# K and V held with 32 keys of two kv-heads per partition, moved by one transfer for each partition quadrant

## The chip, the cores and the metric

The kernel runs on one core of one Trainium2 chip. The metric is device time in microseconds (us), less is better. A core has five engines that run side by side and meet at semaphores: TensorE (PE in the profile, its weight loads PEld), VectorE (DVE), ScalarE (ACT), GpSimd (POOL) and SyncE (SP). Transfers between HBM and the on-chip memory SBUF are issued from a queue of SP, POOL or ACT and are carried out by 16 DMA engines that all queues share. SBUF has 128 partitions; a "quadrant" in this document is a block of 32 partitions in a row (0 to 31, 32 to 63, and so on). Matrix results land in PSUM, from which ACT or DVE copies them to SBUF ("evacuation").

## The reference, cut to what matters

Forward and backward pass of one decode step: attention over a window of a K/V cache and a gated feed-forward net in parallel on the same normalised input, summed with the input.

```python
B, Sq, D = 4, 1, 512
Hq, Hkv, Sk, Dh = 32, 8, 4096, 128          # W = Sk // 4 = 1024 keys are attended
...
q = (xn @ wq).reshape(B, Sq, Hq, Dh).transpose(0, 2, 1, 3)
k = repeat(k_cache[:, :, Sk - W:, :], 4, axis=1)
v = repeat(v_cache[:, :, Sk - W:, :], 4, axis=1)
p = softmax(einsum("bhqd,bhkd->bhqk", q, k) * Dh ** -0.5)
o = einsum("bhqk,bhkd->bhqd", p, v)
out = x + o.reshape(B, Sq, Hq * Dh) @ wo + (gelu(xn @ w_gate) * (xn @ w_up)) @ w_down
# returned: out, and the gradients of x, k_cache, v_cache, wq, wo, w_gate, w_up, w_down
```

The gradients of `k_cache` and `v_cache` (out_2, out_3) have the caches' full shape: 4 batches of 8 heads with 4096 keys. Only the last 1024 keys have a gradient; the 3072 in front of them are written as zeros. All arrays are bfloat16.

## The kernel before, in words

**Data moved.** By the issues of the profile: 32 transfers of 1.5 MB that write zeros, 16 loads of 1 MB (K and V, two for each batch of each), 16 stores of 1 MB (their gradients), 8 stores of 1 MB (gradients of wo and wq), 6 stores of 0.875 MB (gradients of the feed-forward weights), and 13.25 MB of weights.

**Who issues what.** SP loads the weights and the first K tile, and then writes all the zeros. The zeros come from one tile `ztile` that is read on every second partition, 64 of 128, in rows of 12 KB (lines 177 to 180, 228). `zeros(n, after, deep)` (line 236) puts n of these transfers on SP's queue; each waits until the one issued `deep` (2 or 3) before it has landed, and, where `after` is given, until that instruction is done. So zeros are the filler that is dealt out over the kernel. POOL issues the other loads of K and V (`load_kv`, line 216) and every store of a result (`result`, line 112).

**Layout of K and V.** A tile is `[P, G, J, Dh]`: a partition holds J = 8 keys in a row (2 KB) of each of the 8 kv-heads. A load is two transfers, of 4 heads each, over all 128 partitions (lines 219 to 223), put ahead of other work by `tc.high_priority()`. The gradients are staged in the same layout, two staging tiles of 4 heads each, and stored by two transfers over 128 partitions (lines 563 to 565).

**The loop over batches** (lines 613 to 638). For each batch b: `scores(0, b)` turns K on DVE in blocks of 32 by 32 (`t32`, line 91) and multiplies it by the queries, which stand spread out in a tile `bd` that POOL fills (`refill`, line 462); `scores(1, b)` does the same with V and the gradient of the output; `softmax`; `turned` (line 496) transposes the probabilities by matmuls and evacuates them; `odq(0)` (line 567) multiplies them with V; then V of batch b + 1 is loaded; `dvdk(0)` (line 550) forms the gradient of V, evacuates it to two of four staging tiles and stores it; `softmax_d`, `turned`, `odq(1)`; K of batch b + 2 is loaded; `dvdk(1)` does K's gradient. The tile of V has one buffer, so its load waits until `odq(0)` has read the last one.

**Order of the queues.** SP's order is the program's (line 78). POOL's order is found by the scheduler of the framework: a load of K or V goes ahead of stores that stand before it in the program. `evac` (line 82) hands evacuations to ACT or DVE by a running estimate of their load.

**The end.** After the loop come the output, the gradient of x, and the gradients of wo and wq, 4 stores of 1 MB each (lines 715 to 735), with rows of 8 KB in each partition. Rows of the feed-forward gradients have 7 KB.

Of the kernel before, what the change touches and what calls it, by code (L numbers as in the profile page):

```python
# [9 lines left out]
ALU = mybir.AluOpType  # L10
# [4 lines left out]
P = 128  # L15
# [3 lines left out]
def kernel(  # L19
# [54 lines left out]
    stage = ctx.enter_context(tc.tile_pool(name="stage", bufs=4, reuse_waits="tile"))  # L74
# [26 lines left out]
    def stg_tile():  # L101
        return stage.tile([P, 4096], BF16, name="stg", tag="stg")
# [8 lines left out]

    def result(out, in_):
        return store(nc.gpsimd, out, in_, "rest", ["zeros", "rest"], single_packet=True)
# [35 lines left out]
    def mask(name, n, in_):  # L149
# [10 lines left out]
    omt = const.tile([P, NQ, 2], FP32, name="omt")  # L160
    TT(out=omt[:], in0=gmask[:].rearrange("p (c g) -> p c g", g=2), in1=bm[:].unsqueeze(2).broadcast_to([P, NQ, 2]),
       op=ALU.mult)
    om = mask("om", 2, omt[:].rearrange("p c g -> p g c"))
    oms = const.tile([P, 2], FP32, name="oms")
    TS(out=oms[:], in0=om[:], scalar1=scale, scalar2=None, op0=ALU.mult)
    gmask_b = const.tile([P, G], BF16, name="gmask_b")
    nc.vector.tensor_copy(out=gmask_b[:], in_=gmask[:])
    rs2 = const.tile([P, NQ, 4, 8], FP32, name="rs2")
    for c in range(NQ):
        TS(out=rs2[:, c], in0=m8[:].unsqueeze(1).broadcast_to([P, 4, 8]), scalar1=bm[:, c:c + 1], scalar2=None,  # L170
           op0=ALU.mult)
    rs2_f = rs2[:].rearrange("p c a r -> p (c a r)")
    selp = const.tile([P, 4, NQ, 8], BF16, name="selp")
    for a in range(4):
        TS(out=selp[:, a], in0=rs2[:, :, 0, :], scalar1=amask[:, a:a + 1], scalar2=None, op0=ALU.mult)
# [40 lines left out]
    def load_kv(b, k, pool, tag, eng, **kw):  # L216
        d_, src = ((k_t, A_k_cache), (v_t, A_v_cache))[k]
        tl = pool.tile([P, G, J, Dh], BF16, name=tag, tag=tag)
        for hf in range(2):
            hs = slice(hf * G // 2, (hf + 1) * G // 2)  # L220
            with tc.high_priority():
                d = eng.dma_start(out=tl[:, hs].rearrange("p g j d -> p g (j d)"),  # L222
                                  in_=src[b, hs, K0:Sk, :].rearrange("g (m j) d -> m g (j d)", j=J), **kw)
        d_[b] = tl
        return d
# [23 lines left out]
    with tc.tile_pool(name="ffn", bufs=1) as ffn:  # L249
# [74 lines left out]

        dwd_v = out_8.rearrange("(p h c) n -> h p (c n)", h=2, c=FB // 2)
# [11 lines left out]
        for wi, (wsb, dh, og) in enumerate(((wu_sb, dhu, out_7), (wg_sb, dhg, out_6))):  # L337
# [8 lines left out]
            dhs = ffn.tile([P, FPB, 2, 4 * B], BF16, name="dhs", tag=f"dhs{wi}")  # L346
            nc.gpsimd.memset(dhs[:], 0.0)
# [16 lines left out]
            for h in range(2):  # L364
                stg = stg_tile()
                for ci in range(2):
                    for a, q in enumerate(quad):
                        ps = bank("dwg_ps", "w", (P, FQ))
                        mm(ps[:], xn_b[q, 2 * h + ci:D:C], dh_f[q, :], pos=(Q * a, 0))
                        o_ = (ci * NQ + a) * FQ  # L370
                        evac(stg[:, o_:o_ + FQ], ps[:], FQ)
                result(dwg_v[h], stg[:, 0:2 * F])
        nc.vector.tensor_copy(out=dxf[:], in_=dxf_ps[:])

    with tc.tile_pool(name="mid", bufs=1, reuse_waits="tile") as mid:
# [4 lines left out]
        with tc.tile_pool(name="att", bufs=1, reuse_waits="tile") as att:  # L380
            zeros(2, load_kv(0, 1, att, "va", nc.gpsimd, single_packet=True))
            zeros(3, load_kv(1, 0, att, "kb", nc.gpsimd, single_packet=True))

# [4 lines left out]
            for k in range(2):  # L388
                bd.append([])
                for u in range(2):  # L390
                    t_ = att.tile([P, DPB, NQ, 2, 2, Q], BF16, name=f"bd{k}{u}")
                    nc.gpsimd.memset(t_[:], 0.0)
                    bd[k].append(t_)
# [8 lines left out]
            for h in range(Hq):  # L402
                for c in range(C):
# [3 lines left out]
            qs2 = qsc[:, 512:1024].rearrange("p (b c a r) -> p b c a r", b=B, c=NQ, a=4)  # L407
            nc.scalar.activation(out=qs, in_=q_ps[:].rearrange("p h b -> p b h").unsqueeze(2).broadcast_to([P, B, NQ, Hq]),
                                 func=ACT.Copy, scale=scale)
            nc.vector.tensor_copy(out=qs2, in_=qs[:, :, 0, :].rearrange("p b (c r) -> p b c r", c=NQ).unsqueeze(3)  # L410
                                  .broadcast_to([P, B, NQ, 4, 8]))

            def spread_rows(k, get):

                ps = bank("r_ps", "x", (P, B, Dh))
                get(ps, 0)
                rb = scratch()[:].bitcast(BF16)[:, 0:512]
                nc.scalar.copy(out=rb, in_=ps[:].rearrange("p b d -> p (b d)"))
                t32(D3[k][:], pairs(rb), 256)
                ps = bank("r_ps", "x", (P, B, Dh))  # L420
                get(ps, 1)
                nc.scalar.activation(out=rows[k][:, :, 0, :], in_=ps[:], func=ACT.Copy, scale=g2m[:, 0:1])
                TS(out=rows[k][:, :, 1, :], in0=ps[:], scalar1=g2m[:, 1:2], scalar2=None, op0=ALU.mult)

            def get_q(ps, u):
                for b in range(B):
                    l_ = qs[:, b].rearrange("p a h -> p (a h)") if u == 0 else qs2[:, b].rearrange("p c a r -> p (c a r)")
                    mm(ps[:, b, :], l_, ident[:])
# [13 lines left out]
            for u in range(2):  # L442
# [5 lines left out]
            hsel2 = dsc[:, 640:768].rearrange("p (c a r) -> p c a r", c=NQ, a=4)  # L448
            nc.vector.tensor_copy(out=hsel, in_=hm[:].unsqueeze(1).broadcast_to([P, NQ, Q]))
            nc.vector.tensor_copy(out=hsel2, in_=hm[:].rearrange("p (c r) -> p c r", c=NQ).unsqueeze(2)  # L450
                                  .broadcast_to([P, NQ, 4, 8]))
# [4 lines left out]
            def get_d(ps, u):  # L456
                l_ = dsc[:, 512:640] if u == 0 else dsc[:, 640:768]
                mm(ps[:].rearrange("p b d -> p (b d)"), l_, dM.rearrange("p b e k -> p (b e k)"))
# [3 lines left out]
            def refill(k, b):  # L462

                src = D3[k][:].bitcast(BF16).rearrange("p b e (c g i r) -> p b g e c r i", c=NQ, g=2, r=2)
                t_ = bd[k][b % 2]
                for a, q in enumerate(quad):
                    for g2 in range(2):
                        o_ = a * 8 + g2 * 4
                        nc.gpsimd.tensor_copy(out=t_[q, :, :, g2, :, o_:o_ + 4], in_=src[q, b, g2])

            def scores(k, b):
# [4 lines left out]
                for g2 in range(2):  # L476
                    for e in range(2):
                        sc = scratch()
                        t32(sc[:].rearrange("p (c j m) -> p c j m", c=NQ, j=J), src[:, g2:G:2, :, e * Q:(e + 1) * Q], 1024)
                        sb = sc[:].bitcast(BF16).rearrange("p (c n r) -> p c r n", c=NQ, r=2)  # L480
                        for r in range(2):
                            for c, q in enumerate(quad):
                                mm(ps[q, :], t_[:, e, c, g2, r, :], sb[:, c, r, :], g2 == 0 and e == 0 and r == 0,
                                   g2 == 1 and e == 1 and r == 1, (0, Q * c))
# [11 lines left out]
            def turned(src, k):  # L496

                ps = bank("pT_ps", "x", (P, J, Q))
                for j in range(J):
                    for a, q in enumerate(quad):  # L500
                        mm(ps[q, j, :], src[:, j * Q:(j + 1) * Q], selp[:, a].rearrange("p c r -> p (c r)"), pos=(0, Q * a))
                pT = att.tile([P, J, Q], BF16, name="pT", tag=f"pT{k}")
                evac(pT[:], ps[:], NJ)
# [5 lines left out]
            def softmax(S):  # L509
# [4 lines left out]
                mx = small("mx", (1, NQ, 8))  # L514
                nc.vector.reduce_max(out=mx[:], in_=mT_ps[:].rearrange("o (c a r) -> o c r a", c=NQ, a=4), axis=AX.X)
                mx4 = small("mx4", (1, NQ, 4, 8))
                TS(out=mx4[:], in0=mx[:].unsqueeze(2).broadcast_to([1, NQ, 4, 8]), scalar1=-1.0, scalar2=None, op0=ALU.mult)
                nm_ps = bank("nm_ps", "x", (P, 1))
                mm(nm_ps[:], mx4[:].rearrange("o c a r -> o (c a r)"), one_f[:])
# [6 lines left out]
                mm(es_ps[:], rs2_f, es[:])  # L526
# [9 lines left out]
            def softmax_d(P_f, dP):  # L536
# [5 lines left out]
                mm(gs_ps[:], rs2_f, gs[:])  # L542
# [7 lines left out]
            def dvdk(k, b, sp, r_):  # L550

                og = (out_3, out_2)[k]
                stg = [stg_tile() for _ in range(2)]
                sv = [s_[:].rearrange("p (g j d) -> p j g d", g=4, j=J) for s_ in stg]
                for j in range(0, J, 2):
                    ps = [bank("kv_ps", "w", (P, 2, 2, Dh)) for _ in range(NQ)]
                    for u in range(2):
                        for c, q in enumerate(quad):
                            mm(ps[c][:, u].rearrange("p g d -> p (g d)"), sp[q, j + u].rearrange("p a m -> p (a m)"),
                               r_[q, b].rearrange("p g d -> p (g d)"), pos=(Q * c, 0))  # L560
                    for c in range(NQ):
                        evac(sv[c // 2][:, j:j + 2, (c % 2) * 2:(c % 2) * 2 + 2, :], ps[c][:], 512)
                for hf in range(2):
                    result(og[b, hf * 4:(hf + 1) * 4, K0:Sk, :].rearrange("g (m j) d -> m g (j d)", j=J),
                           stg[hf][:].rearrange("p (g e) -> p g e", g=4))

            def odq(k, b, pT):
# [3 lines left out]
                for j in range(J):  # L571
                    for c, q in enumerate(quad):
                        mm(ps[q].rearrange("p g d -> p (g d)"), pT[:, j, :], src[:, 2 * c:2 * c + 2, j, :],
                           j == 0, j == J - 1, (0, Q * c))
                mk = (om, oms)[k]
# [190 lines left out]
```

## Time and profile before

| | |
|---|---|
| time, median of 3 runs | 284.86 us (283.6 to 286.5) |
| the profiled execution: its own time, its span | 284.82 us, 283.0 us |
| busy: PE, DVE, ACT, POOL | 187.6, 165.0, 124.4, 60.3 us |
| moved by the 16 DMA engines | 112.21 MB |
| POOL's 30 stores: busy, idle before them | 19.7 us, 150.0 us |
| POOL's 14 loads of K and V: busy in all, mean | 10.5 us, about 0.75 us |

The span runs from the first to the last instruction; the execution's own time has 1.8 us around it. "DMA share" in a table of stretches is the share of the 16 engines' time in which they carry packets; a value a little over 1 comes from packets that begin inside the stretch and end behind it. "GB/s" is what they moved in it. In the chain of waits each line gives a start, a length, and what the end was waiting for.

### The profile page before, as it was taken

To read this page: it belongs to the slowest core of one execution; us is meant where nothing else is said; L and a number is where in the kernel's file an instruction comes from. 1 tells how busy PE (TensorE), PEld (TensorE's weight loads), DVE (VectorE), ACT (ScalarE), POOL (GpSimd) and SP (SyncE) were. 2 spreads that over 40 slices of the span, in tenths; PEclk is the share of its full clock that TensorE was granted. 3 is DMA by queue.
4 is the path that set the end of the run, shared out by engine and by line. 5 is a ranking of instruction groups with operands and counts; after the bars stand their busy time and mean duration, and the time that the engine had idled before them with its cause. 6 is when DMAs were issued, how large, how long until landed. Compare 5 with 4: busy or idle time off the path is not lost.

```text
span 283.0 us, 4400 instructions
## 1 busy us (share of the span) xinstructions
PE 187.6 (66%) x1731; PEld 76.8 (27%) x1733; DVE 165.0 (58%) x309; ACT 124.4 (44%) x245; POOL 60.3 (21%) x135
## 2 busy tenths in 40 slices
PE   0225989859544899759976663923357998944870
PEld 0102344233111543234331341311034232510210
DVE  4779674898798533635257254055496104396970
ACT  2032774740010469744725420802432767454870
POOL 8500000169075313120040060200020020201110
PEclk9999965556955555755555555555555555685555
DMA  6999989999999999999999999999999999999995
GB/s 217 430 446 435 432 317 420 424 430 396 392 428 406 383 357 425 328 365 411 421 419 414 408 427 405 396 422 421 429 382 423 413 410 403 399 415 396 391 397 223
DMA packets 16883, 112.21 MB, mean 396 GB/s; under 512 B 1368, under 2 KB 1632, under 8 KB 11104
## 3 DMA queue, kind: packets, MB, share of 16 engines
q1 hardware_dynamic: 6544, 66.46, 57.0%
q0 software_dynamic: 10176, 45.35, 40.8%
q8 instruction: 13, 0.21, 0.3%
q10 hardware_dynamic: 144, 0.13, 0.2%
q14 instruction: 6, 0.05, 0.0%
HBM read 30.93 MB, written 81.01 MB: 396 GB/s over the span
## 4 chain that ended last, share of the span: by engine, by line
DMA 30%; issue 14%; PE 13%; DVE 9%; ACT 3%; POOL 2%; POOLq 0%; ACTq 0%; DVEq 0%
DMA out_dram<-stg 30%; DVE scr L93 4%; PE kv_ps L117 4%; PE od_ps L117 3%; PE sc_ps L117 2%; PE dwq_ps L117 2%; ACT stg L88 2%; DVE stg L89 1%; POOL out_dram L106 1%; PE ok_ps L117 1%; PE es_ps L117 1%; DVE spr L492 1%; DVE dqs L593 1%; ACT E_f L524 1%; PE nm_ps L117 1%
## 5 line engine op out<-in xcount | busy, mean ns | idle before, releaser
L88 ACT CAST stg<-kv_ps 128x512 bf16<-128x512 f32 x118 | 63.6, 606 | 52.2 <-DMA out_dram<-stg 26.3
L106 POOL DMA_DIRECT2D out_dram<-stg x30 | 19.7, 659 | 150.0 <-ACT stg L88 94.7
L117 PE MATMUL sc_ps<-scr,bd 128*32 128x256 bf16 x256 | 24.2, 396 | 15.2 <-DVE scr L93 15.2
L117 PE MATMUL kv_ps<-qm,spr 32*128 32x256 bf16 x128 | 24.8, 385 | 13.0 <-ACT stg L88 12.5
L117 PE MATMUL kv_ps<-dm,spr 32*128 32x256 bf16 x128 | 28.9, 399 | 6.6 <-ACT stg L88 4.9
L93 DVE STREAM_TRANSPOSE scr<-va 128x1024 uint32<-128x1024 uint32 x16 | 18.9, 1219 | 12.9 <-DMA va<-in_A_v_cache_dram 12.8
L117 PEld LDWEIGHTS <-spr 32*128 32x128 bf16 x256 | 12.4, 102 | 46.4 <-issue 42.1
L89 DVE CAST stg<-kv_ps 128x512 bf16<-128x512 f32 x10 | 6.6, 683 | 17.0 <-PE kv_ps L117 11.0
L117 PEld LDWEIGHTS <-bd 128*32 128x32 bf16 x256 | 8.1, 107 | 29.1 <-issue 28.5
L88 ACT CAST stg<-dwg_ps 128x448 bf16<-128x448 f32 x26 | 12.7, 554 | 6.4 <-PE dwg_ps L117 5.5
L88 ACT CAST stg<-dwo_ps 128x512 bf16<-128x512 f32 x18 | 10.0, 588 | 11.4 <-PE dwo_ps L117 10.1
L117 PE MATMUL dwo_ps<-dy_b,oSP 32*128 32x512 bf16 x32 | 9.0, 508 | 7.5 <-ACT stg L88 6.2
L93 DVE STREAM_TRANSPOSE scr<-ka 128x1024 uint32<-128x1024 uint32 x8 | 9.6, 1228 | 5.2 <-DMA ka<-in_A_k_cache_dram 3.1
L222 POOL DMA_DIRECT2D va<-in_A_v_cache_dram x8 | 6.0, 757 | 27.3 <-PE od_ps L117 25.8
L93 DVE STREAM_TRANSPOSE scr<-kb 128x1024 uint32<-128x1024 uint32 x8 | 9.8, 1232 | 3.5 <-DMA kb<-in_A_k_cache_dram 2.9
L117 PE MATMUL do_ps<-scr,dyBD 128*128 128x512 bf16 x31 | 10.1, 459 | 2.4 <-DVE scr L93 2.1
L578 DVE SCALAR_TENSOR_TENSOR odt<-od_ps,oms,odt 128x128 f32<-128x128 f32 x4 | 1.4, 340 | 17.0 <-ACT odt L577 17.0
L117 PE MATMUL dwq_ps<-dqSP,xn_b 32*128 32x512 bf16 x32 | 10.7, 586 | 0.9 <-ACT stg L88 0.3
L89 DVE CAST stg<-dwq_ps 128x512 bf16<-128x512 f32 x15 | 9.9, 689 | 1.6 <-PE dwq_ps L117 1.4
L89 DVE CAST stg<-dwo_ps 128x512 bf16<-128x512 f32 x14 | 9.2, 680 | 2.7 <-PE dwo_ps L117 2.7
L117 PEld LDWEIGHTS <-pT 128*32 128x32 bf16 x256 | 9.2, 140 | 5.2 <-ACT pT L88 2.3
L88 ACT CAST stg<-dwq_ps 128x512 bf16<-128x512 f32 x17 | 9.7, 586 | 1.4 <-PE dwq_ps L117 0.7
(196 smaller groups left out, 321.3 us busy)
## 6 DMA issues: line engine op xcount, KB each, us to landing
out_dram<-ztile SPq DMA_DIRECT2D x32, 1536.0 KB, 12.1
out_dram<-stg POOLq DMA_DIRECT2D x24, 1024.0 KB, 13.7
va<-in_A_v_cache_dram POOLq DMA_DIRECT2D x8, 1024.0 KB, 17.6
out_dram<-stg POOLq DMA_DIRECT2D x6, 896.0 KB, 10.2
wq_sb<-in_A_wq_dram SPq DMA_DIRECT2D x1, 4096.0 KB, 25.6
wo_sb<-in_A_wo_dram SPq DMA_DIRECT2D x1, 4096.0 KB, 36.7
kb<-in_A_k_cache_dram POOLq DMA_DIRECT2D x4, 1024.0 KB, 19.4
ka<-in_A_k_cache_dram SPq DMA_DIRECT2D x2, 1024.0 KB, 44.3
```

Of the source, the lines that this page charges most:

```text
L88: return nc.scalar.copy(out=out, in_=in_)
L89: return nc.vector.tensor_copy(out=out, in_=in_)
L93: nc.vector.transpose(out=out, in_=in_)
L106: d = eng.dma_start(out=out, in_=in_, **kw)
L117: nc.tensor.matmul(out, lhsT=lhsT, rhs=rhs, start=first, stop=last, **kw)
L222: d = eng.dma_start(out=tl[:, hs].rearrange("p g j d -> p g (j d)"), in_=src[b, hs, K0:Sk, :].rearrange("g (m j) d -> m g (j d)", j=J), **kw)
L492: TS(out=sp[:, :, a, :], in0=src[:].rearrange("p (j m) -> p j m", j=J), scalar1=amask[:, a:a + 1], scalar2=None, op0=ALU.mult)
L524: nc.scalar.activation(out=E_f[:], in_=S, func=ACT.Exp, bias=negm[:, 0:1], scale=1.0, accum_out=es[:])
L578: done = STT(out=t_[:], in0=ps[:, 1, :], scalar=mk[:, 1:2], in1=t_[:], op0=ALU.mult, op1=ALU.add)
L593: nc.vector.tensor_copy(out=dqs[q, :, :, :, a * B + b], in_=d3v[q])
```

## The change

K and V and their gradients get another layout. A tile is now `[P, 2, Q, Dh]`: quadrant c holds heads 2c and 2c + 1, and a partition holds 32 keys in a row (8 KB) of each of the two. HBM and SBUF then agree only inside a quadrant, so a tile moves by one transfer for each quadrant: 512 KB each on SP's queue and for the stores, and 256 KB each (one head) for POOL's loads. A tile's load on POOL is 8 transfers where it was 2, on SP 4 where it was 2, and a gradient's store is 4 where it was 2.

What follows from the layout: the masks `om`, `rs2` and the second spread of the rows fall away; `refill` is two multiplications by a mask on POOL in place of 8 small copies, and the `bd` tiles need no clearing; `turned` ends in one DVE multiplication by a mask from PSUM to a tile four times as large, in place of an evacuation; `selp` is built by 16 small DVE operations in place of 4.

What is changed beside it: every DMA that POOL issues is chained behind the one before it in the order of the program, without a semaphore, and `tc.high_priority()` is gone; the last store of the feed-forward gradients is moved behind the first two loads of POOL, and two clearings on POOL (`dhs`) stand earlier; the staging buffer is one tile with four parts in place of a pool of four.

```diff
-    stage = ctx.enter_context(tc.tile_pool(name="stage", bufs=4, reuse_waits="tile"))
+    stage = ctx.enter_context(tc.tile_pool(name="stage", bufs=1))
...
-    def stg_tile():
-        return stage.tile([P, 4096], BF16, name="stg", tag="stg")
+    stg_all = stage.tile([P, 4, 4096], BF16, name="stg")
+    stg_next = [0]
+    def stg_tile(n=1):
+        k = stg_next[0] = -(-stg_next[0] // n) * n
+        stg_next[0] += n
+        return stg_all[:, k % 4] if n == 1 else stg_all[:, k % 4:k % 4 + n]
...
+    pool_dma = []
+    def in_order(d):
+        if pool_dma:
+            tc.add_manual_dep(d.ins, pool_dma[-1].ins.name,
+                              mybir.DependencyInfo(mybir.DependencyClass.NoSync, mybir.DependencyReason.DATA))
+        pool_dma.append(d)
     def result(out, in_):
-        return store(nc.gpsimd, out, in_, "rest", ["zeros", "rest"], single_packet=True)
+        in_order(store(nc.gpsimd, out, in_, "rest", ["zeros", "rest"], single_packet=True))
...
     def load_kv(b, k, pool, tag, eng, **kw):
-        tl = pool.tile([P, G, J, Dh], BF16, name=tag, tag=tag)
-        for hf in range(2):
-            hs = slice(hf * G // 2, (hf + 1) * G // 2)
-            with tc.high_priority():
-                d = eng.dma_start(out=tl[:, hs].rearrange("p g j d -> p g (j d)"),
-                                  in_=src[b, hs, K0:Sk, :].rearrange("g (m j) d -> m g (j d)", j=J), **kw)
+        tl = pool.tile([P, 2, Q, Dh], BF16, name=tag, tag=tag)
+        for g0, gn in ((0, 2),) if eng is nc.sync else ((0, 1), (1, 1)):
+            for c, q in enumerate(quad):
+                d = eng.dma_start(out=tl[q, g0:g0 + gn].rearrange("p g j d -> p g (j d)"),
+                                  in_=src[b, 2 * c + g0:2 * c + g0 + gn, K0:Sk, :]
+                                  .rearrange("g (m j) d -> m g (j d)", j=Q), **kw)
+                if eng is nc.gpsimd:
+                    in_order(d)
...
             def refill(k, b):
-                for a, q in enumerate(quad):
-                    for g2 in range(2):
-                        o_ = a * 8 + g2 * 4
-                        nc.gpsimd.tensor_copy(out=t_[q, :, :, g2, :, o_:o_ + 4], in_=src[q, b, g2])
+                for g2 in range(2):
+                    nc.gpsimd.tensor_tensor(out=bd[k][b % 2][:, g2], in0=src[:, b],
+                                            in1=hmask[:, g2].unsqueeze(1).unsqueeze(1).broadcast_to([P, DPB, 2, Q]),
+                                            op=ALU.mult)
...
             def turned(src, k):
-                pT = att.tile([P, J, Q], BF16, name="pT", tag=f"pT{k}")
-                evac(pT[:], ps[:], NJ)
+                load["dve"] += 1200
+                pT = att.tile([P, J, NQ, NQ, 8], BF16, name="pT", tag=f"pT{k}")
+                TT(out=pT[:].rearrange("p j a c r -> p (j a) c r"),
+                   in0=ps[:].rearrange("p j (a r) -> p (j a) r", a=NQ).unsqueeze(2).broadcast_to([P, J * NQ, NQ, 8]),
+                   in1=bm[:].unsqueeze(1).unsqueeze(3).broadcast_to([P, J * NQ, NQ, 8]), op=ALU.mult)
...
             def dvdk(k, b, sp, r_):
-                stg = [stg_tile() for _ in range(2)]
+                stg = stg_tile(2)
+                sv = stg.rearrange("p g (j d) -> p j g d", j=Q)
...
-                for hf in range(2):
-                    result(og[b, hf * 4:(hf + 1) * 4, K0:Sk, :].rearrange("g (m j) d -> m g (j d)", j=J),
-                           stg[hf][:].rearrange("p (g e) -> p g e", g=4))
+                for c, q in enumerate(quad):
+                    result(og[b, 2 * c:2 * c + 2, K0:Sk, :].rearrange("g (m j) d -> m g (j d)", j=Q), stg[q])
```

## The prediction

> **What bounds the kernel now.** I read the busy shares of the page first. No engine reaches 70%, so I went on to its DMA lines:
>
> ```profile
> PE 187.6 (66%) x1731; PEld 76.8 (27%) x1733; DVE 165.0 (58%) x309; ACT 124.4 (44%) x245; POOL 60.3 (21%) x135
> ...
> DMA  6999989999999999999999999999999999999995
> GB/s 217 430 446 435 432 317 420 424 430 396 392 428 406 383 357 425 328 365 411 421 419 414 408 427 405 396 422 421 429 382 423 413 410 403 399 415 396 391 397 223
> DMA packets 16883, 112.21 MB, mean 396 GB/s; under 512 B 1368, under 2 KB 1632, under 8 KB 11104
> ...
> q1 hardware_dynamic: 6544, 66.46, 57.0%
> q0 software_dynamic: 10176, 45.35, 40.8%
> ```
>
> The reader is to see the row of nines: outside the first and the last slice the 16 DMA engines are never free. q1 is SP's queue (weights, zeros), q0 is POOL's (K, V, all results). Their shares add up to 97.8% of the span. So the end is set by bytes divided by the rate at which busy DMA engines move them, and a change counts by that rate or by leaving the engines without work.
>
> Second, the chain of waits, to see whether anything else stands in a row with it, and what SP waits for:
>
> ```profile
> 127.03 23.70 DMA out_dram<-stg
> ...
> 164.87 36.97 DMA out_dram<-stg
> ```
>
> ```profile
> SPq L106 <- DMA out_dram<-ztile: 127.1, 21, 14.5
> ...
> SPq L106 <- DMA va<-in_A_v_cache_dram: 23.2, 4, 9.2
> SPq L106 <- DMA ka<-in_A_k_cache_dram: 13.3, 1, 13.3
> ```
>
> The loop's longest pieces are evacuations waiting for a staging tile that a store still reads (60.7 us in two pieces). Compute waits for DMA, and has that much slack. SP's zeros wait for older zeros, or for a K/V tile to land.
>
> Third, a table of stretches, chosen for what was in flight in each, for the rate that busy engines reach. Columns: stretch and length, then busy time and count by engine, granted PE clock, DMA share and GB/s.
>
> ```profile
> 95.00:99.00 4.00, 3.68 (x50) 2.57 (x43) 2.31 (x7) 1.75 (x4) 1.66 (x3) 0.50 0.96 406
> ...
> 102.00:104.40 2.40, 2.40 (x35) 0.83 (x34) 0.42 (x1) 1.75 (x3) 0.92 (x4) 0.50 0.99 399
> 116.40:118.40 2.00, 1.70 (x12) 0.47 (x11) 1.77 (x4) 1.28 (x3) 0.76 (x1) 0.50 0.96 283
> ...
> 266.00:278.00 12.00, 8.29 (x25) 1.68 (x23) 8.39 (x13) 7.83 (x14) 2.13 (x4) 0.50 0.95 389
> 58.00:256.00 198.00, 137.82 (x1369) 59.41 (x1370) 108.85 (x203) 84.45 (x172) 43.96 (x107) 0.55 1.00 404
> 256.00:283.00 27.00, 14.76 (x47) 3.16 (x44) 15.17 (x23) 14.10 (x25) 3.74 (x7) 0.50 0.86 352
> ```
>
> ```profile
> 114.00:124.00 10.00, 6.51 (x86) 3.09 (x88) 5.64 (x16) 6.15 (x14) 0.76 (x1) 0.60 0.94 316
> ```
>
> 95 to 99 is zeros alone (12 KB rows, every second partition): 406 at share 0.96, so 423 GB/s of a full share. 102 to 104.4 is a load of V alone (2 KB rows): 399/0.99 = 403. 266 to 278 is stores with 8 KB rows: 389/0.95 = 409. The stretch 114 to 124 is the one to remember: K/V loads and stores meet there, the engines are full (0.94), and only 316 GB/s come out, in its worst two microseconds 283. So full engines can be held up by what they reach into.
>
> **The change part by part.** K, V and their gradients are 32 transfers of 1 MB, 33.55 MB. At the loop's 404 GB/s they take 83.0 us of the span.
>
> *Longer rows.* 33.55 MB at 403 (2 KB rows) are 83.3 us, at 409 (8 KB rows) 82.0: gain 1.2 us. At the best rate of any row kind, 423, they are 79.3: gain 4.0. A loss is excluded, as the row with the longer rows is no slower. I take 1.2, the row with just these rows; 4.0 stays as the end.
>
> *32 partitions per transfer.* Every transfer of the trace with some size to it touches at least 64 partitions, spread from first to last. Now each works inside one block of 32, and POOL issues the quadrants in turn, so the DMA engines work on the same block at the same time. No row shows that. Lower end: 0, as zeros on half of the partitions still run at 423. Upper end: the worst stretch with full engines, 283 GB/s: 33.55/0.283 = 118.6 us, +35.6. Between them lies the ten-microsecond stretch of K/V traffic, 316: 106.2 us, +23.2. I take +23.2: this stretch is K/V traffic held up with full engines, while the zeros' row is of a spread access that the change gives up. The loss lies on the path, since DMA is the bound and nothing hides it.
> [...]
>
> *More issues on POOL.* 14 loads at 0.75 us (10.5) become 56, 16 stores at 0.75 (12.0) become 32. Each has 32 or 64 rows; the stores of 128 rows at the end took 0.53 to 0.55. At 0.53: 29.7 + 17.0 = 46.7 us, +24.2 on an engine busy 60.3 of 283.0 that idles 150.0 before its stores. Nothing lies on the path as long as the DMA engines have transfers queued, and they do: a zero transfer is in flight 12.1 us, a store 13.7. What is late: a tile's last part is issued at 8 x 0.53 = 4.2 us in place of 1.5, so 2.7 later. Behind the waiting load stand POOL's stores, and SP's zeros that wait for the landing.
>
> *Program order on POOL.* Loads in the loop now stand behind the four stores of the gradient before (2.1 us), where at 125.5 and 162.6 the load went first. Five loads in the loop come 2.1 + 2.7 = 4.8 us later. In return a store is no longer held by a load that waits (at 111.55 the load preceded a store by 1.5 us). Cover: zeros and stores in flight, as above: 0 taken. Without cover 5 x 4.8 = 24 us; a gain is possible only by the 1.5 us per store.
>
> *Moved pieces.* The last feed-forward store behind the loads and the earlier `dhs` clearing are the order that the trace already had (loads at 58.1 and 60.3, store at 61.8, clearing at 8.9): 0. SP's K load is 4 issues in place of 2, about +1.0 us before the first zero, with 13 MB of weights queued: 0.
>
> *Compute.* `turned`: ACT's copy of 0.40 us becomes a DVE product of 1024 columns; the nearest row (the end's product with a mask, 128x1024) took 1.22. 8 x 0.8 = +6.6 us of latency between probabilities and `odq`. `refill`: 64 copies at 0.23 (14.7) become 16 products; between 0.23 and 1.0 us (a clearing of 1024 columns) each, 4 to 16 us; four clearings of 0.97 go. `selp`, `om`, `rs2`: some 16 small DVE operations at 0.24 for 8, +2 us while the first weights load. The second spread of the rows (about 2 us of matmuls, a 0.28 us copy) goes. All of it lies beside DMA, under the 60.7 us of slack; it costs 6.6 us only if that goes.
>
> *Sum.* 283.0 + 23.2 - 1.2 = 305.0 us of span, + 1.8 around it = 306.8. The profiled execution is 284.82, as good as the median 284.86, so no more is to be corrected.
>
> **The rivals.**
>
> *A, other side: the block of partitions costs nothing.* Four quadrants are in POOL's queue within 2.1 us, SP's packets go between them, and DMA engines may run apart so that the blocks mix. For: zeros at 423 on half the partitions. Against: 114 to 124. Time: 283.0 - 1.2 + 1.8 = 283.6; with the gain of 4.0, 280.8, and if packets of 8 KB let K/V finish sooner and zeros fill the end (27 us at share 0.86, at most 3.8 us), 277. It decides if K/V alone keeps more than about 395 GB/s.
>
> *B: DMA runs out of work.* Rate unchanged, but later loads hold SP's zeros (23.2 + 13.3 us of such waits now). 4.8 us on five loads is 24 uncovered; a third to all gives 283.6 + 8 = 292 to 308. For: `zeros` behind a load wait for its last part. Against: share 1.00 over 58 to 256. It decides when the share there falls under 0.96.
>
> *C: the block halves the rate outright.* K/V at half of 404 are 166.1 us, +83.1: 366.7. For: the same two stretches. Against: no row is as slow as that with full engines. It decides if K/V alone falls to 200 GB/s and nothing mixes the blocks.
>
> **How the numbers follow.** Chances: mine 0.48 (299 to 326: bounds 23.2 and 35.6, with up to 8 of B), A 0.34, B 0.14, C 0.04. A splits into 0.21 faster by over 1% (under 282.0) and 0.13 within 1%, which is about what a measurement here can tell from no change; B gives 0.01 of "same". So faster 0.21, same 0.14, slower 0.65. The range, 279.5 to 326, leaves out A's lowest part, C and the top of mine, some 0.15. The likeliest case's own range is 299 to 326.
>
> **What would show it.** Right: DMA share stays near 1.00 in the loop, GB/s there falls towards 340 to 370, q0's share of 16 engines' time per MB rises, waits for `out_dram<-stg` grow. Row length: q0's packets fall well under 10176, and those "under 8 KB" from 11104 to a few thousand. Wrong: GB/s at 404 or above in the loop with full engines (A), or a share under 0.96 with SP waiting for loads (B); a chain led by DVE or PE would mean that I overlooked compute.

## The result, and the profile after

The changed kernel takes 329.0 us (median of 4 runs, 326.7 to 332.3) against 285.7 for the kernel before beside it (283.6 to 286.8): ratio 1.150, 95% interval 1.138 to 1.162. It is slower, as forecast, but by 43 us where 22 were predicted, and 3 us above the upper end of the range. The profiled execution took 327.8 us, with a span of 325.7. Times here and below are medians of all runs of a kernel, while a ratio, and the differences in us that are named with it, leave out runs over 1.5% above the kernel's fastest.

From the page of the changed kernel, the DMA lines that stand against those of before:

```profile
DMA  6999999999999999999999999999899999999960
GB/s 259 426 446 443 319 399 425 424 384 229 345 426 401 250 261 358 390 302 414 345 333 373 332 316 412 322 320 305 208 289 297 314 320 387 424 427 430 425 287 14
DMA packets 13235, 112.22 MB, mean 345 GB/s; under 512 B 2328, under 2 KB 2592, under 8 KB 3360
...
q1 hardware_dynamic: 5808, 66.46, 50.6%
q0 software_dynamic: 7264, 45.36, 44.9%
```

The bytes are the same and the row of nines is still there, but the mean fell from 396 to 345 GB/s. The dips (229, 250, 208) stand where K, V or their gradients move; in the feed-forward part in front and beside the weight gradients behind, most slices still reach 424 to 446. The packets are fewer and longer, as the layout says.

Shares of the page times the span give engine time. Before: q0 0.408 x 283.0 = 115.5 us, q1 0.570 x 283.0 = 161.3. After: 0.449 x 325.7 = 146.2 and 0.506 x 325.7 = 164.8. So POOL's packets cost 30.7 us more, SP's 3.5: 34 of the 42.7 us are packets that took longer. The other 8.5 are time in which engines carry nothing, most of it at the end.

Stretches of the changed kernel (length, busy time and count of PE, PEld, DVE, ACT and POOL, granted PE clock, DMA share, GB/s): the loop, a stretch of loads, a stretch of gradients and zeros, and the end.

```profile
58.00:256.00 198.00, 127.84 (x1368) 54.56 (x1368) 112.22 (x197) 77.34 (x164) 55.41 (x113) 0.59 1.00 334
66.00:82.00 16.00, 8.98 (x30) 2.92 (x28) 12.92 (x18) 1.17 (x2) 5.87 (x12) 0.82 1.02 299
206.00:245.00 39.00, 27.06 (x365) 12.21 (x365) 12.82 (x27) 17.13 (x36) 4.08 (x9) 0.68 0.95 286
310.00:323.00 13.00, 0.00 (x0) 0.00 (x0) 0.00 (x0) 0.00 (x0) 0.00 (x0) 0.50 0.40 170
```

The first line answers the 404 GB/s of before: still share 1.00, now 334. The last shows the end: share 0.40, though the last transfer was issued at 303.7 us. The trace has 16 packets in flight at 309 us, some 10 at 315 and 2 at 319, so some of the 16 engines are through with their part long before the others. SP's waits in the changed kernel:

```profile
SPq L112 <- DMA out_dram<-ztile: 207.4, 25, 27.9
SPq L112 <- DMA va<-in_A_v_cache_dram: 25.7, 3, 12.7
```

Zeros wait for older zeros 207 us in place of 127, for loads of V hardly longer (25.7, before 23.2): the queue is not held up by later loads, its transfers last longer (18.3 us from issue to landing, before 12.1). The longest pieces of the chain are of the same kind as before, evacuations waiting for a store that still reads a staging tile (23.8 and 36.2 us).

### The profile page after: what moved, and what is told of

It reads as the page before. It is cut to its first block, busy times and chain, and to the rows that moved or that the text cites. A ratio compares the mean times of both kernels' runs of the same rounds, so it can differ in the third digit from the quotient of the medians.

```text
span 325.7 us, 4475 instructions
## 1 busy us (share of the span) xinstructions
PE 181.6 (56%) x1726; PEld 72.8 (22%) x1728; DVE 170.8 (52%) x314; ACT 121.9 (37%) x247; POOL 72.1 (22%) x141
## 3 DMA queue, kind: packets, MB, share of 16 engines
q0 software_dynamic: 7264, 45.36, 44.9%
## 4 chain that ended last, share of the span: by engine, by line
DMA 50%; DVE 17%; PE 14%; ACT 5%; issue 4%; POOL 2%; POOLq 0%; ACTq 0%; DVEq 0%
DMA out_dram<-stg 31%; DMA va<-in_A_v_cache_dram 8%; DVE scr L93 7%; DMA kb<-in_A_k_cache_dram 6%; DMA ka<-in_A_k_cache_dram 5%; ACT stg L88 3%; PE kv_ps L132 2%; PE do_ps L132 2%; PE od_ps L132 2%; PE da_ps L132 1%; PE dwg_ps L132 1%; PE dwo_ps L132 1%; POOL va L234 1%; PE h_ps L132 1%; DVE pT L510 1%
## 5 line engine op out<-in xcount | busy, mean ns | idle before, releaser
L112 POOL DMA_DIRECT2D out_dram<-stg x46 | 24.6, 536 | 158.9 <-ACT stg L88 107.5
L132 PE MATMUL kv_ps<-qm,spr 32*128 32x256 bf16 x128 | 29.8, 392 | 8.1 <-ACT stg L88 8.1
L132 PE MATMUL sc_ps<-scr,bd 128*32 128x256 bf16 x256 | 19.4, 403 | 16.7 <-DVE scr L93 10.8
L132 PE MATMUL kv_ps<-dm,spr 32*128 32x256 bf16 x128 | 24.5, 371 | 4.2 <-ACT stg L88 2.3
L132 PE MATMUL dwo_ps<-dy_b,oSP 32*128 32x512 bf16 x32 | 11.1, 578 | 23.0 <-ACT stg L88 22.9
L234 POOL DMA_DIRECT2D va<-in_A_v_cache_dram x32 | 15.8, 498 | 31.1 <-DMA out_dram<-stg 13.6
L88 ACT CAST stg<-dwo_ps 128x512 bf16<-128x512 f32 x21 | 11.1, 612 | 23.0 <-DMA out_dram<-stg 22.2
L89 DVE CAST stg<-dwo_ps 128x512 bf16<-128x512 f32 x11 | 7.2, 687 | 22.4 <-DMA out_dram<-stg 12.2
L234 POOL DMA_DIRECT2D kb<-in_A_k_cache_dram x16 | 7.9, 497 | 24.8 <-DMA out_dram<-stg 12.8
L533 ACT ACTIVATE E_f<-sc_ps,negm 128x256 f32<-128x256 f32 x4 | 2.1, 520 | 22.3 <-DVE negm L530 22.3
## 6 DMA issues: line engine op xcount, KB each, us to landing
out_dram<-ztile SPq DMA_DIRECT2D x32, 1536.0 KB, 18.3
```

The costliest lines, as they stand in the source:

```text
L88: return nc.scalar.copy(out=out, in_=in_)
L89: return nc.vector.tensor_copy(out=out, in_=in_)
L112: d = eng.dma_start(out=out, in_=in_, **kw)
L132: nc.tensor.matmul(out, lhsT=lhsT, rhs=rhs, start=first, stop=last, **kw)
L234: d = eng.dma_start(out=tl[q, g0:g0 + gn].rearrange("p g j d -> p g (j d)"), in_=src[b, 2 * c + g0:2 * c + g0 + gn, K0:Sk, :] .rearrange(" ...
L533: nc.scalar.activation(out=E_f[:], in_=S, func=ACT.Exp, bias=negm[:, 0:1], scale=1.0, accum_out=es[:])
```

## The experiments

The theory: a transfer confined to 32 neighbouring partitions is slow by itself, whatever its rows, while all 16 engines count as busy. Against it stood the other parts of the change: 8 KB rows, the number of transfers on POOL, its program order, and the compute. Diffs are against the kernel after unless another is named.

**Rates of one kind of transfer.** A kernel that computes nothing: it only moves 4 MB or so a stage on POOL's queue, each stage behind the one before.

```diff
+    ABCD = (0, 1, 2, 3, 0, 1, 2, 3)
+    ACBD = (0, 2, 1, 3, 0, 2, 1, 3)
...
+        stage(quads(a, 1, store, ABCD))
+        stage(quads(a, 2, store, ACBD))
+        stage([(part(0, 1, 32, 2 * i), rows8(z, 0, i // 4, 2 * (i % 4)), store) for i in range(8)])
+        stage(spread(z, 1, store))
```

`quads` moves two rows of 8 KB on each partition of the quadrants listed, `part(0, 1, 32, ...)` the same on quadrant 0 alone, and `spread` on partitions i, i + 4, i + 8 and so on.

> Leaves out the whole computation: only transfers on POOL's queue, nothing beside them, in stages that wait for each other; first loads, then the same as stores, 4 MB each: 128 partitions with 2 KB rows; 128 partitions with 8 KB rows; quadrants in the order 0,1,2,3 twice; quadrants 0,2,1,3 twice; quadrant 0 eight times; 32 partitions that lie 4 apart, eight times; 128 partitions with 2 KB rows again. Theory 1, the block of 32 neighbouring partitions is what slows: both 128-partition rows near 400 GB/s, quadrant 0 alone near 200, the order 0,1,2,3 between 200 and 300, the 32 partitions 4 apart near 400; the order 0,2,1,3 is higher than 0,1,2,3 if the limit belongs to a half of the partitions and DMA engines spread over two transfers. Rival 2, the queue on POOL and its order: every stage near 400, with the quadrant stages at most some per cent lower for their issues. Rival 3, the 8 KB rows: the 128-partition stage with 8 KB rows is as slow as the quadrants.

Stretches inside the stages (busy DVE and POOL, clock, DMA share, GB/s). Loads: 128 partitions with 8 KB rows; quadrants 0, 1, 2, 3; quadrants 0, 2, 1, 3; quadrant 0 alone; 32 partitions, each fourth; 128 partitions with 2 KB rows. Then stores: 128 partitions with 8 KB rows; quadrants in order; 0, 2, 1, 3; quadrant 0 alone; 32 partitions, each fourth; 128 with 2 KB rows.

```profile
28.00:38.00 10.00, 6.88 (x1) 0.82 (x2) 1.00 0.97 398
42.00:60.00 18.00, 0.00 (x0) 2.17 (x5) 1.00 1.02 216
66.00:80.00 14.00, 0.00 (x0) 0.89 (x2) 1.00 1.02 219
88.00:105.00 17.00, 0.00 (x0) 1.07 (x3) 1.00 1.01 204
110.00:119.00 9.00, 0.00 (x0) 2.30 (x5) 1.00 1.01 419
124.00:133.00 9.00, 0.00 (x0) 0.34 (x1) 1.00 1.02 393
151.00:159.00 8.00, 0.00 (x0) 0.22 (x1) 1.00 1.01 409
165.00:176.00 11.00, 0.00 (x0) 0.80 (x2) 1.00 0.97 250
184.00:196.00 12.00, 0.00 (x0) 2.04 (x4) 1.00 0.95 324
200.00:217.00 17.00, 0.00 (x0) 2.21 (x5) 1.00 0.98 202
222.00:231.00 9.00, 0.00 (x0) 3.27 (x7) 1.00 1.00 404
236.00:244.00 8.00, 0.00 (x0) 0.77 (x2) 1.00 1.01 366
```

The reader is to see the last two columns together: at the same share of about 1.0 the engines move 204 or 419 GB/s with the same number of partitions and the same 8 KB rows. It is not the number of partitions (32) but that they are neighbours. Loads through the quadrants in turn stay at 216; stores reach 250, and 324 in the order 0, 2, 1, 3, as a mean over a stage that begins at 209 and reaches 426 in its last microseconds. The rival of the long rows falls too: over 128 partitions 8 KB rows move 398 and 409.

**The same beside zeros.** A kernel that computes nothing: in each stage SP issues 4 transfers of zeros, and POOL 4 MB beside them.

> Leaves out the whole computation. Each stage puts 4 transfers of zeros (6.3 MB) on SP's queue and beside them 4 MB on POOL's: nothing; stores over 128 partitions (2 KB rows); stores by quadrants in order; stores from 32 partitions that lie 4 apart; loads over 128; loads by quadrants; loads to 32 partitions 4 apart; nothing. Theory 1a, the limit belongs to a direction (reads of SBUF meet reads): the stage with quadrant stores is the slowest, with long zero packets too (below 330 GB/s), the one with quadrant loads loses less, because zeros only read. Theory 1b, the limit belongs to the block in both directions alike: both quadrant stages equally slow. Both: the stages with 128 partitions and with 32 partitions 4 apart near 400.

Stretches with the same columns. Zeros alone; with stores over 128 partitions; by quadrant; by each fourth partition; with loads over 128; by quadrant; the rest of those loads when the zeros were through; loads by each fourth partition.

```profile
40.00:53.00 13.00, 0.00 (x0) 0.00 (x0) 1.00 1.01 423
58.00:76.00 18.00, 0.00 (x0) 0.85 (x2) 1.00 1.00 398
88.00:112.00 24.00, 0.00 (x0) 0.35 (x1) 1.00 1.00 307
126.00:142.00 16.00, 0.00 (x0) 0.00 (x0) 1.00 1.02 425
152.00:168.00 16.00, 0.00 (x0) 0.00 (x0) 1.00 0.99 404
184.00:200.00 16.00, 0.00 (x0) 0.00 (x0) 1.00 1.01 419
201.00:206.00 5.00, 0.00 (x0) 0.00 (x0) 1.00 0.97 205
216.00:230.00 14.00, 0.00 (x0) 0.00 (x0) 1.00 1.01 426
```

Zeros and stores both read SBUF, and a store by quadrant costs beside zeros what it costs alone: 6.3 MB at 423 and 4.2 MB at 202 to 250 one after the other would be 294 to 331 GB/s, 307 came out. A load by quadrant writes SBUF, and beside zeros the engines still move 419; its price shows only when the zeros have ended (205). Why the two directions differ, no run shows.

**One part undone.** Both directions, the loads alone, the stores alone go back to two transfers over 128 partitions; masks, products, program order and staging stay changed.

```diff
-            for c, q in enumerate(quad):
-                d = eng.dma_start(out=tl[q, g0:g0 + gn]...)
+        for hf in range(2):
+            d = eng.dma_start(out=tl[:, hf].rearrange("p (g j) d -> p g (j d)", g=4), ...)
...
-                for c, q in enumerate(quad):
-                    result(og[b, 2 * c:2 * c + 2, K0:Sk, :]..., stg[q])
+                for hf in range(2):
+                    result(og[b, hf * 4:(hf + 1) * 4, K0:Sk, :]..., stg[:, hf]...)
```

> The changed kernel with K's and V's loads and their gradients' stores put back to two transfers over 128 partitions with 2 KB rows; the rest of the change stays (masks, products, program order on POOL, one staging tile), so keys and heads land in the wrong places and the results are not the reference's. Theory 1 (block of partitions): the whole loss is gone, 283 to 288 us. Rival 2 (program order on POOL and what else was changed): it stays above 300, since all of that is still in.

286.3 us, ratio 1.000 (0.997 to 1.004), 286.0 for the kernel before beside it. Its stretches:

```profile
58.00:256.00 198.00, 136.90 (x1358) 55.36 (x1352) 112.79 (x201) 89.03 (x177) 34.10 (x57) 0.54 1.00 402
66.00:82.00 16.00, 8.50 (x55) 3.16 (x54) 14.54 (x20) 1.18 (x2) 3.31 (x8) 0.80 1.02 411
```

The whole loss is gone with the form of the transfers: masks, products, program order, staging together cost nothing that can be measured.

> The changed kernel with only the loads of K and V put back to two transfers over 128 partitions with 2 KB rows (data in wrong places, results not the reference's); the stores stay by quadrants. Theory 1: K/V loads are half of the 33.55 MB, so about half of the 43 us comes back, 300 to 315 us, more if loads are the worse half. Rival 2 (waits between POOL's many loads): most of it comes back, 285 to 292, since 56 issues become 14.

323.0 us, 1.120 (1.112 to 1.129): with only the stores by quadrant 34 us of the loss remain. The loop:

```profile
58.00:256.00 198.00, 128.11 (x1337) 52.98 (x1336) 106.13 (x187) 77.31 (x161) 38.38 (x70) 0.57 0.95 332
```

> The changed kernel with only the stores of the gradients of K and V put back to two transfers over 128 partitions with 2 KB rows (data in wrong places, results not the reference's); the loads stay by quadrants. Theory 1: about half of the 43 us comes back, 300 to 315 us. Rival 2: little comes back, above 318, since the many loads on POOL stay.

299.1 us, 1.045 (1.038 to 1.052): with only the loads by quadrant 13 us remain.

```profile
58.00:256.00 198.00, 137.47 (x1378) 54.70 (x1378) 110.56 (x193) 84.99 (x174) 51.97 (x98) 0.56 1.01 388
```

I had expected about half of the loss from each, 300 to 315 us in both runs, and missed both, the second by 1 us. The stores carry most of it; the measurement beside zeros fits that, as the zeros run beside nearly everything and read SBUF too (307 GB/s with stores by quadrant, 419 with loads). 34 and 13 are 47, which the intervals, 2 to 3 us on each side, don't separate from 43.

**Another order of the quadrants.** `for c in (0, 2, 1, 3)` for loads and stores.

> The changed kernel with the quadrants issued 0, 2, 1, 3 in loads and stores. Transfers alone in this order gave 220 GB/s for loads, as slow as in order, and for stores up to 413 once DMA engines had drifted apart. Theory 1: little to some gain, 310 to 328 us, since a queue is worked off transfer by transfer. Rival (neighbouring issues share a half, so the order is the flaw): 290 to 300.

318.9 us, 1.111 (1.103 to 1.118): some 11 us come back, in line with the 324 against 250 of the stores alone in that order. Loads alone gained next to nothing from it (219 against 216).

**Stores that touch all quadrants.** Same 8 KB rows, same number of transfers, same layout in HBM; only the partition that holds a head's keys changes, so that a store reads every fourth partition.

```diff
-                sp = att.tile([P, J, 4, Q], BF16, name="spr", tag=f"spr{k}")
+                sp = att.tile([P, J, Q, 4], BF16, name="spr", tag=f"spr{k}")
-                    TS(out=sp[:, :, a, :], ...)
+                    TS(out=sp[:, :, :, a], ...)
...
-                            mm(..., sp[q, j + u].rearrange("p c m -> p (c m)"),
+                            mm(..., sp[q, j + u].rearrange("p m c -> p (m c)"),
...
-                for c, q in enumerate(quad):
-                    result(og[b, 2 * c:2 * c + 2, K0:Sk, :]..., stg[q])
+                for c in range(NQ):
+                    result(og[b, 2 * c:2 * c + 2, K0:Sk, :]..., stg[c:P:4])
```

> The changed kernel, where only the order of the columns of the spread probabilities is turned, so that a head pair's gradient lies in every fourth partition and a store reads 32 partitions from all four quadrants; rows of 8 KB, number of transfers, their order and all else as in the changed kernel. Theory 1: the stores' part of the loss is gone, as when they went over 128 partitions: 295 to 302 us (that run had 299). Rival (the number of stores, their 512 KB, the long rows): stays at 320 to 330.

296.6 us, 1.037 (1.031 to 1.043): 32 of the 43 us are back. Its stretches:

```profile
76.00:84.00 8.00, 0.39 (x1) 0.10 (x1) 5.43 (x11) 1.18 (x2) 4.94 (x8) 0.65 1.02 235
206.00:245.00 39.00, 30.71 (x375) 13.56 (x375) 16.84 (x33) 17.21 (x37) 4.39 (x8) 0.62 1.01 426
58.00:256.00 198.00, 134.57 (x1379) 56.44 (x1378) 117.20 (x199) 82.29 (x175) 59.53 (x114) 0.56 1.01 394
```

The stretch of gradients and zeros, 286 GB/s in the changed kernel, runs at 426. A part of what is left lies where loads by quadrant run without zeros beside them (235). By the page's shares its packets cost (0.545 + 0.414) x 294.0 = 281.9 us, 5 more than the (0.570 + 0.408) x 283.0 = 276.8 of the kernel before. Its span is 11 longer, so the other 6 are time in which engines carry nothing.

**Long rows over 128 partitions.** Whole heads with 8 KB rows are loaded by two transfers over 128 partitions (other keys than the reference attends to), stores are over 128.

```diff
+        for hf in range(2):
+            d = eng.dma_start(out=tl[:, hf].rearrange("p j d -> p (j d)"),
+                              in_=src[b, hf].rearrange("(m j) d -> m (j d)", j=Q), **kw)
```

> The changed kernel with stores over 128 partitions (2 KB rows) and with loads over 128 partitions in rows of 8 KB, each a whole head of the cache (other data, wrong places, results not the reference's). It shows what longer rows bring by themselves on half of the K/V bytes, beside the run with 2 KB rows for both (286). By the transfers alone, 429 against 376 GB/s at best: 16.8 MB in 39 against 45 us, a gain of up to 5 us, 281 to 286 us. Rival (row length is worth nothing beside zeros): 286 within 1.

289.2 us, 1.012 (1.007 to 1.017), where 281 to 286 were expected. Its packets cost (0.554 + 0.397) x 287.2 = 273.1 us, 3 less than with 2 KB rows in both directions ((0.567 + 0.402) x 285.0 = 276.2), but the time is 3 us (1%) higher, and the two ratios' intervals don't meet. The longer rows are worth packet time, and something else costs more than that; 1.2 us of it come at the end (see the next run), the rest is open.

**The number of transfers.** The kernel before, with 8 loads for a tile on POOL (4 on SP) and 4 stores for a gradient, all over 128 partitions with 2 KB rows.

```diff
-        for hf in range(2):
-            hs = slice(hf * G // 2, (hf + 1) * G // 2)
+        n_ = 4 if eng is nc.sync else 8
+        for hf in range(n_):
+            hs = slice(hf * G // n_, (hf + 1) * G // n_)
```

> The kernel before with the changed kernel's number of transfers: a K or V tile is loaded by 8 transfers of one head on POOL (4 on SP), a gradient is stored by 4 of two heads, all still over 128 partitions with 2 KB rows. Theory 1 (only the block of partitions costs): at most the longer closing of POOL, some 3 us, 285 to 291 us. Rival 2 (number of transfers and POOL's waits between them): 295 to 325.

Ratio 1.025 (1.017 to 1.033), from runs of 290.4 to 294.4 us: some 7 us, a little over what was expected.

I had expected the number to show in POOL's closing, the long last wait of its program, behind its last store. It ends after SP's by 0.34 us in the kernel before and in the changed one with all transfers over 128 partitions (44 transfers on POOL each), by 1.49 with long rows (44), 2.14 with only the stores by quadrant (60), 2.8 in the next run (74), 3.06 with only the loads by quadrant (86) and 3.72 in the changed kernel (102). The number is not the reason: with 102 transfers in 2 KB rows the trace of this kernel, of an execution of 350 us, has 0.37. The closing is long in the kernels that move K, V or their gradients in rows of 8 KB; whether by the rows or by the fewer partitions isn't taken apart.

POOL's loads also begin to wait for older transfers of POOL itself. In the changed kernel the loads of V stand 13.6 us and those of K (`kb`) 12.8 us behind stores from `stg`, which read no buffer of a load. No run shows why; the trace with as many transfers in 2 KB rows has no such wait of a load. What the 7 us are made of is open.

**Fewer loads in the spread version**: 4 loads of 512 KB for a tile, `for g0, gn in ((0, 2),)`, against the spread kernel.

> The changed kernel with stores from every fourth partition, and with a K or V tile loaded by 4 transfers of 512 KB on POOL in place of 8 of 256 KB. Theory 1 (loads that run alone are held to 210 GB/s): the block is the same and stays longer in one half, 295 to 302 us, no better than 296.6. Rival 2 (waits between POOL's many loads): 286 to 292.

294.7 us, 1.033 (1.028 to 1.038): some 1 to 2 us less, not separable from none by the intervals. It is the best time with the new layout and rows of 8 KB.

**Zeros beside the loads.** Since loads by quadrant are free beside zeros, the zeros were released earlier: by an instruction in front of the load, not by its landing. Four kernels have it: the spread version, the kernel before as a control, the kernel after, and the spread version with only the five zeros in front of the loop.

```diff
-                    zeros((2, 2, 4)[b], load_kv(b + 1, 1, att, "va", nc.gpsimd, single_packet=True))
+                    load_kv(b + 1, 1, att, "va", nc.gpsimd, single_packet=True)
+                    zeros((2, 2, 4)[b], o_done)
...
```

> The changed kernel with stores from every fourth partition, and with SP's zeros in the loop and in front of it released by the instruction that frees the tile (the end of the output product, or the copy of the input gradient) in place of the landing of the load, so that zeros run beside the loads. Theory 1a (loads by quadrants are slow only where they have the DMA engines to themselves: 210 GB/s alone, 418 beside zeros): the remaining 11 us go, 283 to 288 us, or to 280 if longer rows bring something. Rival (loads by quadrants are slow whatever runs beside them): 294 to 298, no change.

> The kernel before with the same release of the zeros as above, as its control. Theory 1a: loads over 128 partitions run at 400 GB/s with or without zeros beside them, so nothing changes, 284 to 287 us. Rival (any kernel gains when zeros run beside loads): 280 or less, and what the run above gains says nothing of quadrants.

> The changed kernel with nothing but the release of the zeros as above; stores stay by quadrants. Theory 1a: the loads' part of some 11 us goes, the stores' part of some 33 us stays or grows, since zeros and quadrant stores read the same side: 312 to 322 us. Rival (loads' order on POOL is the cost): 325 to 331.

> The changed kernel with stores from every fourth partition, where only the five zeros in front of the loop are released by the copy of the input gradient in place of the landing of the first V and K loads; in the loop they stay as they were. Theory 1: the first two tiles' loads run beside zeros at full rate, which gives back up to 4.2 MB at 210 against 400 GB/s, some 9 us at best, 288 to 294 us, if the zeros are not missed later. Rival: 295 or more.

Measured: spread 298.9 us (1.044, 1.038 to 1.050), control 303.8 (1.056, 1.050 to 1.063), after 332.9 (1.153, 1.143 to 1.162), five zeros 302.2 (1.058, 1.051 to 1.064). None gained, and all four expectations were missed. The control tells why; its loop, and below it that of the spread version:

```profile
58.00:256.00 198.00, 118.17 (x1165) 50.50 (x1156) 92.87 (x173) 72.81 (x150) 40.26 (x102) 0.54 0.90 362
```

```profile
58.00:256.00 198.00, 134.10 (x1374) 56.87 (x1373) 113.27 (x193) 79.20 (x169) 58.09 (x113) 0.57 0.96 388
```

In the kernel before, the early release alone costs 16 us: the share in the loop falls from 1.00 to 0.90. From 58 to 95 us the engines are as full as before (1.01), and from 95 to 113, where the kernel before had zeros and a load of V (1.01), their share is 0.35, from 190 to 206 it is 0.73: some 16 us of engine time in all. The filler is spent while other transfers were there anyway, and is missing later. In the spread version the packets cost (0.534 + 0.391) x 298.3 = 275.9 us, back at the 276.8 of before, so loads beside zeros are free in the kernel too; the gain is eaten by idle engines (share 0.96).

**Half of the loads from ACT's queue**, in the spread version: quadrants 2 and 3 by `nc.scalar.dma_start`.

> The changed kernel with stores from every fourth partition, and with the loads of quadrants 2 and 3 issued from ACT's queue, those of 0 and 1 from POOL's, so that two transfers in different halves are in flight side by side. [...]

309.2 us, 1.072 (1.064 to 1.080): worse. Where nothing but loads from the two queues was in flight, from 66 to 73 and from 108 to 115 us, the engines moved 262 and 245 GB/s at share 1.02, little more than the 235 of one queue and far from the 398 of loads over 128 partitions alone. The issuing also holds up ACT: four loads of K took it 8.3 us from 63.0 us on, and its next instruction began at 71.4. SP's zeros wait for V 62.5 us in all (31.0 in the spread version).

## Why the prediction was right and wrong

*The bound and the direction* were right. DMA engines stayed full (1.00 over the loop), so the time went with their rate, and the rate fell, to 334 GB/s where 340 to 370 were foretold. The waits changed as foretold: those of ACT's and DVE's evacuations for `out_dram<-stg` grew from 34.3 to 80.7 us.

*32 partitions per transfer* is the term that failed, in its size. The prediction took +23.2, "this stretch is K/V traffic held up with full engines", with 35.6 as the bound. Nothing but the partitions that a store reads brought back 32 us, and the loads that stayed in quadrants cost some 5 us of packets: about 37 together, the bound and a little more. That the bound came so close is chance. The stretch of 316 GB/s was traffic over 128 partitions, slowed by something that no run took apart, and had no bearing on a block of 32; nor does it show, as the prediction concluded, that full engines are held up by what they reach into. Alone, one quadrant moves 202 to 204 GB/s, under every row I had, and loads through the quadrants 216 to 219. That the loss was not larger still is a matter of direction: loads pay only while no zeros run (205 GB/s, beside zeros 419), stores pay nearly in full (307 beside zeros). The prediction's +23.2 did not tell the two apart.

*Longer rows*, -1.2: q0's packets fell from 10176 to 7264 as foretold, and those of the loads cost 3 us less over 128 partitions; no time came of it (289.2 against 286.3).

*More issues on POOL*, 0: the second term that failed, +7 (5 to 9) by the run that changes only their number. I had counted issue time (0.50 us a load, 0.54 a store, close to the 0.53 of the prediction) against POOL's idle time, and that is not what costs. What does is open; POOL's closing isn't it.

*Program order, moved pieces, compute*, 0: right (1.000 with all of them in place).

*Rivals.* A (a block costs nothing) fell: 202 to 204 GB/s alone. B (engines without work) fell for this kernel: the loop's share is 1.00, and the 8.5 us of idle time lie mostly at the end, where nothing waits to be issued. B came true only where I released zeros early (shares of 0.90 and 0.96). C (half rate) is what a quadrant does alone, and its condition, that nothing mixes the blocks, is not met (stores through the quadrants moved 250 and 324): 329 us, not 366.7.

*Open*: of the spread version's last 11 us, 5 are packets, by the zeros' early release those of lone loads, and 6 are idle engines, nearly all of them at the end, with 3.4 for POOL's later closing. How that fits with the 7 us for the number of transfers alone isn't known: fewer loads gave at most 2. No version beat the kernel before.

## What to carry to other kernels

Let each transfer touch partitions of all four quadrants, every fourth if it has but 32, before caring for row length: alone, 2 KB rows over 128 partitions moved 366 to 393 GB/s, 8 KB rows on every fourth partition 404 to 419, in one quadrant 202 to 204 and through the quadrants in order 216 to 250. Read the DMA share and the GB/s of a stretch together, and ask which other transfers go in the same direction at that time (beside zeros, stores by quadrant 307 GB/s, loads by quadrant 419). A row that merely looks like the new traffic is no price for it: if no row has the new access pattern, the range must reach to the time that a far lower rate, here half, would give, or a small measurement of that pattern alone must come first.

## What the runs showed of the hardware

- Busy engines need not move much: share 1.02 with 216 GB/s, share 1.02 with 425.
- What counts is that the 32 partitions are neighbours: 202 to 204 GB/s in one quadrant, 404 to 419 on every fourth partition.
- Beside zeros the slowdown goes by direction: quadrant stores 307 GB/s, quadrant loads 419.
- POOL's closing ended 0.34 us after SP's with 44 transfers in 2 KB rows and 0.37 with 102; it was 1.49 to 3.72 where K, V or their gradients moved in rows of 8 KB.
- Two queues that loaded into different halves of the partitions moved 245 to 262 GB/s together.
- The 16 engines can finish far apart: share 0.40 in the changed kernel's last 13 us of transfers.
